# A chained attention and two expert layers on one core: the second weights' splits, the one-hots, the last tile and the last expert's gathers are moved

## The chip, the core and the metric

One Trainium2 chip, one of its cores, one launch. The metric is the device time of one execution in microseconds (us); lower is better. The profile below was taken by the hardware profiler in one execution of its own.

## What is computed

Three stages, each fed by the one before, all in float32 (inputs as numpy arrays):

```python
# 1. clustered attention: batch 2, 8 heads, 768 positions, 64 wide, 16 clusters a head
q_assign = argmax(q_n @ c_n.T); k_assign = argmax(k_n @ c_n.T)
scores = where(q_assign == k_assign, scale * q @ k.T, -1e9)
attn_out = softmax(scores) @ v
x = attn_out.transpose(0, 2, 1, 3).reshape(1536, 512)
# 2. experts, top 2 of 8, with noise on the gate
noisy = x @ w_gate + log1p(exp(x @ w_noise)) * noise
for each token, its two best experts e with softmax weight g:
    out += g * (relu(x @ w1[e]) @ w2[e])          # w1 512 x 1024, w2 1024 x 512
# 3. experts, top 1 of 8, at most 384 tokens an expert
probs = softmax(x @ w_gate2); e = argmax
out = probs[e] * (relu(x @ w1[e]) @ w2[e])        # tokens beyond the capacity stay 0
```

## The kernel before

**Arithmetic.** Float32 products are made of two rounded words: each operand is split into a high word (`hh`, `wh`, `xh`: a copy by ScalarE that rounds) and a low word (`hl`, `wl`, `xl`: VectorE subtracts the high one), and three matmuls (high x high, high x low, low x high) are added in one accumulator. So every weight that arrives (`raw`, 128 x 1024 at a time) is split by one ScalarE activation (L202) and one VectorE subtraction (L203). A "half" is one expert's w1 or w2; it has four such chunks. Half 0 is expert 0's w1, half 1 its w2, half 2 expert 1's w1, and so on. Four staging buffers hold raw chunks, three buffers of split words (`WB`) take the halves in turn.

**Attention.** 16 heads (2 batches of 8), each in six tiles of 128 queries, software-pipelined by a table of slots (`SLOTS`): scores, maximum, exponential, transposition, product with v into one accumulator `acc` in PSUM (half a head at a time, copied out to `oT` at L825), and `xback`, which turns the result back, scales it (`xp`) and adds the head's share of the gate logits to `LG`. In the last heads half 0 is split in pieces (`wneed0` at the steps listed in `WS`), the rows of the first job are gathered, and its first hidden chunk (`wide1` with f = 0) is made at a fixed step.

**Jobs.** Each expert is a job: gather the rows of its tokens by indirect DMA on GpSimd (`gathers`), turn and split them (`prep`), first matmul in eight hidden chunks of 128 (`wide1`, 12 matmuls each; ScalarE makes `hh`, VectorE `hl`), second matmul tile by tile of 128 rows (`second`, 24 matmuls of 512 columns over the eight hidden chunks), copy out (`y`), scatter by indirect DMA (`scatter`, L1195). Expert 0 is two jobs, `jobs[0]` with 256 rows of batch 0 and `jobs[1]` with 256 rows of batch 1; so is the last expert (jobs 8 and 9). Job 0 can run before batch 1 is routed.

**Routing of batch 1** (`route1(1)`) runs beside job 0 as a generator: job 0 calls `tick` after each group of matmuls, and a tick lets the generator emit so many steps (`us` times a pace; `PA` is the pace during job 0's first matmul, 3.0). It finds the two best experts of each token (A, L395), ranks the tokens by matmuls with triangular and all-one matrices (`ranks`, L298 to L303), turns ranks into slots, makes 12 pairs of one-hot matrices on VectorE (`ohp` 128 x 128, `ohv` 128 x 96, L321 and L323), multiplies them into a table on TensorE (L447) and finishes it (L449, then L329 to L337) to the token list `t1k`, which job 1's gathers (L1044) read. `K0` to `K3` space these steps.

Each engine takes its instructions in the order in which the program emits them. `wneed(n)` emits all splits that are left up to half n; `wneed0(n)` emits one. Until job 1's gathers are issued, no further weights are fetched (`rush`); the first fetch after that waits for the gathered rows. `early` issues the next job's gathers when its list is there; `fill` emits the next job's `prep`, once the planner's clock has passed the due time of its rows (`GT` after the gathers).

`first` fetches, for a last-expert job, the rows that its tokens got from their other expert (`y_dram`, L1214) and their gate weights (`g_dram`), which ScalarE multiplies (L1220). `combine` adds the two experts' rows of a token (L1652, L1653) and stores them (L1656) beside job 8. `every[-1]` is the last job of the third stage; its second and last tile stands in a branch on the count of its rows.

The lines of `work` that the change reorders:

```python
        early()
        if job.last:
            job.first()
...
                if job is jobs[0] and f % 2 == 0:
                    wneed0(1)
                tick(12 * job.n / 2400, PA if job is jobs[0] else 3.0)
...
        wneed(job.h + 1)
```

## Time and profile before

| | us |
|---|---|
| median of three runs | 857.37 (853.73 to 858.87) |
| the profiled execution | 849.86 |
| its span, first to last instruction | 848.1 |
| TensorE busy in it | 820.2 |
| VectorE, ScalarE, GpSimd busy | 540.1, 495.1, 287.9 |

Times in the views are counted from the span's start. PE is TensorE, DVE VectorE, ACT ScalarE, POOL GpSimd, SP SyncE; an engine's name with a q is its queue of instructions that only issue. A timeline row is start, duration, engine, source line, operation, output <- input, shape, count, and in brackets the engine's idle time just before it with what ended that. Matmuls overlap their neighbours, so the step from one start to the next is their cost, and a row's duration is longer than that.

### The profile page before, as it was taken

The numbers are of one execution on the slowest core, as the hardware profiler recorded it, in microseconds if no ns is written. First come the engines' busy times: TensorE is split into PE (matmuls) and PEld (weight loads), VectorE is DVE, ScalarE is ACT, GpSimd is POOL, SyncE is SP. The second block draws the span as 40 slices with busy tenths as digits, with TensorE's granted clock in tenths as the row PEclk, the third lists the DMA queues.
The fourth block names the chain that finished last, engine by engine and source line by source line (L and its number), as shares of the span: only waits on it lengthen the run. The fifth ranks groups of instructions, "written<-read, shape, count | busy, mean of one in ns | idle before, by whom it ended". The sixth has DMA issues, their size and how long they took to land. (4 is left out here: it accounts for less than half of the span.)

```text
span 848.1 us, 14830 instructions
## 1 busy us (share of the span) xinstructions
PE 820.2 (97%) x5350; PEld 733.6 (87%) x5350; DVE 540.1 (64%) x1104; ACT 495.1 (58%) x959; POOL 287.9 (34%) x488
## 2 busy tenths in 40 slices
PE   8999999999998989999999999999999999999997
PEld 6999999888987868989888897988997789888895
DVE  7998888889988666447444443536476548565370
ACT  7989889888888315435343343436254347555461
POOL 3565565667764031231302021124322122222210
PEclk9999999999999999999999999999999999999999
DMA  3125521411113034744644454438465529775250
GB/s 97 34 72 181 198 73 33 147 46 50 39 39 111 20 138 152 241 161 137 185 157 138 166 150 137 119 138 275 144 222 181 191 80 295 274 233 183 87 166 18
DMA packets 62181, 116.75 MB, mean 138 GB/s; under 512 B 13737, under 2 KB 25769, under 8 KB 62096
## 3 DMA queue, kind: packets, MB, share of 16 engines
q1 hardware_dynamic: 52832, 92.60, 34.4%
q0 software_dynamic: 9264, 23.06, 8.1%
q8 instruction: 47, 0.77, 0.4%
q14 instruction: 38, 0.31, 0.1%
HBM read 97.29 MB, written 23.74 MB: 143 GB/s over the span
## 5 line engine op out<-in xcount | busy, mean ns | idle before, releaser
L203 DVE TENSOR_TENSOR wl<-raw,wh 128x1024 fp32r<-128x1024 f32 x124 | 150.3, 1222 | 44.9 <-ACT wh L202 42.5
L1106 PE MATMUL l<-xh,wh 128*128 128x256 f32 (+1 forms) x508 | 156.0, 309 | 2.3 <-ACT xh L1087 0.9
L1106 PE MATMUL l<-xh,wl 128*128 128x256 f32 (+1 forms) x508 | 155.4, 308 | 0.2 <-DVE wl L203 0.2
L1106 PE MATMUL l<-xl,wh 128*128 128x256 f32 (+1 forms) x508 | 148.1, 307 | 0.0
L1151 PE MATMUL l<-wh,hh 128*128 128x512 f32 x328 | 134.9, 411 | 1.5 <-PEq L1343 0.5
L202 ACT ACTIVATE wh<-raw 128x1024 fp32r<-128x1024 f32 x124 | 129.0, 1054 | 7.9 <-DMA raw<-in_moe_w_dram 6.9
L1153 PE MATMUL l<-wh,hl 128*128 128x512 f32 x328 | 129.3, 394 | 0.0
L1152 PE MATMUL l<-wl,hh 128*128 128x512 f32 x328 | 129.0, 393 | 0.0
L1109 DVE SCALAR_TENSOR_TENSOR hl<-l,hh 128x256 fp32r<-128x256 f32 (+1 forms) x127 | 61.3, 484 | 98.6 <-ACT hh L1108 96.4
L1108 ACT ACTIVATE hh<-l 128x256 fp32r<-128x256 f32 (+1 forms) x127 | 55.0, 433 | 101.5 <-PE l L1106 99.6
L801 DVE TENSOR_TENSOR El<-et,Eh 128x384 fp32r<-128x384 f32 x192 | 99.7, 550 | 11.1 <-ACT Eh L800 8.1
L1106 PEld LDWEIGHTS l<-xh,wh 128*128 128x128 f32 x508 | 95.6, 188 | 5.8 <-issue 2.8
L1106 PEld LDWEIGHTS l<-xh,wl 128*128 128x128 f32 x508 | 95.4, 188 | 1.1 <-DVE wl L203 0.4
L769 DVE TENSOR_REDUCE nm<-st 128x1 f32<-128x768 f32 x96 | 91.3, 951 | 6.0 <-PE st L764 4.9
L1106 PEld LDWEIGHTS l<-xl,wh 128*128 128x128 f32 x508 | 93.7, 188 | 0.6
L800 ACT ACTIVATE Eh<-et 128x384 fp32r<-128x384 f32 x192 | 87.2, 493 | 10.5 <-PE et L795 10.2
L778 ACT ACTIVATE E<-st,nm 128x768 f32<-128x768 f32 x96 | 87.1, 907 | 7.6 <-DVE nm L769 7.6
L1195 POOL DMA_INDIRECT y_dram<-y,t1d x23 | 23.2, 1010 | 195.5 <-ACT y L1174 157.5
L1153 PEld LDWEIGHTS l<-wh,hl 128*128 128x128 f32 x328 | 61.6, 188 | 14.9 <-DVE hl L1123 0.3
L1151 PEld LDWEIGHTS l<-wh,hh 128*128 128x128 f32 x328 | 61.8, 188 | 14.6 <-issue 3.1
L795 PE MATMUL et<-identr,Er 128*128 128x128 f32 x576 | 70.9, 241 | 1.1 <-DVE El L801 1.0
L763 PE MATMUL st<-KB,QC 80*128 80x384 f32 x192 | 70.6, 367 | 1.2 <-ACT E L778 1.2
(331 smaller groups left out, 1527.5 us busy)
## 6 DMA issues: line engine op xcount, KB each, us to landing
raw<-in_moe_w_dram SPq DMA_DIRECT2D x128, 512.0 KB, 4.4
vraw<-in_v_dram SPq DMA_DIRECT2D x16, 192.0 KB, 2.5
x_dram<-xp SPq DMA_DIRECT2D x8, 384.0 KB, 3.2
out_dram<-xg SPq DMA_DIRECT2D x1, 3072.0 KB, 9.9
y_dram<-xg SPq DMA_DIRECT2D x1, 3072.0 KB, 9.9
part<-y_dram SPq DMA_DIRECT2D x12, 256.0 KB, 4.2
yt<-y_dram SPq DMA_DIRECT2D x12, 256.0 KB, 4.4
x_dram<-part POOLq DMA_DIRECT2D x12, 256.0 KB, 4.4
```

Source lines behind the costliest of these rows:

```text
L202: nc.scalar.activation(wh[:, cs], raw[0], AF.Copy)
L203: nc.vector.tensor_tensor(wl[:, cs], raw[0], wh[:, cs].bitcast(F32), op=OP.subtract)
L763: nc.tensor.matmul(ps, st["QC", i][:64 + C, js], st["KB", i][:64 + C, cs], start=True, stop=False)
L769: nc.vector.tensor_reduce(nm, ps, axis=AX.XY, op=OP.max, negate=True)
L778: made = nc.scalar.activation(E, st.pop(("S", i, j))[:, :, :HW], AF.Exp, bias=st.pop(("nm", i, j)), accum_out=st["Z", i][:, j:j + 1])
L795: ins = nc.tensor.transpose(ps[:, n * 128:(n + 1) * 128].bitcast(F32R), E[:, part, n * 128:(n + 1) * 128], identr)
L800: nc.scalar.activation(Eh[o], ps, AF.Copy)
L801: nc.vector.tensor_sub(El[o], ps, Eh[o].bitcast(F32))
L1106: nc.tensor.matmul(ps[:, :n], (w1l if k == 2 else w1h)[:, c, fs], (self.xl if k == 1 else self.xh)[:, c, :n], start=(m == 0), stop=(m == l ...
L1151: nc.tensor.matmul(ps[:rows], hh[:, f, cs], w2h[:, f, :], start=(f == 0), stop=False)
L1152: nc.tensor.matmul(ps[:rows], hh[:, f, cs], w2l[:, f, :], start=False, stop=False)
L1153: nc.tensor.matmul(ps[:rows], hl[:, f, cs], w2h[:, f, :], start=False, stop=(f == FC - 1))
```

## The change

1. Split weights are kept in tiles that hold half of the words of a half, high and low together (`wtile`, `Half`), and the tile for the first two chunks of half 1 is there from the start (`WB[1]`).
2. Job 0's first hidden chunk is emitted when the next to last half head of the attention is done, and the first two chunks of half 1 are split on either side of it; the third is split just ahead of the one-hots, the fourth just after the token table.
3. For batch 1 the ranks stand behind hidden chunk 5 (`FR`), the steps from the ranks to the one-hots are emitted in one go, and of the 12 pairs of one-hots six `ohv` are made on ScalarE, as relu(code - 2 code (lane - f)^2). The table matmuls stand behind the first four hidden chunks of both tiles in job 0's second matmul, which goes by parts of the hidden chunks (`second_turns`: four, two, two) and not tile by tile. The pace `PA` is 4.5.
4. For head 15 `xback` adds the gate logits first, on VectorE, and scales the rows after that.
5. The last tile of the last job is made in two column halves of 256; each is copied out by ScalarE and VectorE, 128 columns each, and scattered by itself.
6. In a last-expert job, `first` stands ahead of `early`.

The diff, cut to its core:

```diff
-    F0, FP, T0, PA = 1, (2, 4), 1.5, 3.0
-    K0, K1, K2, K3 = 10, 3, 1.5, 2
...
+    class Half:
+        def __init__(self, tiles, k, nch):
+            self.tiles, self.k, self.per = tiles, k, nch // 2
+        def __getitem__(self, key):
+            _, c, fs = key
+            w = self.tiles[c // self.per][:, self.k].rearrange("p (c f) -> p c f", c=self.per)
+            return w[:, c % self.per, fs]
+    def wtile(pool, p, n):
+        return pool.tile([128, 2, 2048], F32R, name=f"w{p}{n}")
+    WB = [[wtile(ring, p, 0) for p in "ab"], [wtile(ring, "a", 1)]]
...
             def op(cs=cs, raw=raw, g=g):
-                wh, wl = WB[buf]
-                W[n] = [w.rearrange("p (c f) -> p c f", c=nch) for w in (wh, wl)]
-                nc.scalar.activation(wh[:, cs], raw[0], AF.Copy)
-                nc.vector.tensor_tensor(wl[:, cs], raw[0], wh[:, cs].bitcast(F32), op=OP.subtract)
+                W[n] = [Half(WB[buf], p, nch) for p in range(2)]
+                wh, wl = [WB[buf][g // 2][:, p, cs] for p in range(2)]
+                nc.scalar.activation(wh, raw[0], AF.Copy)
+                nc.vector.tensor_tensor(wl, raw[0], wh.bitcast(F32), op=OP.subtract)
...
-    def one_hot(f, n, code, ncol):
-        oh = rt.tile([128, 128], F32R, name="ohp", bufs=4)
+    def one_hot(f, n, code, ncol, pool=None, minus=None):
+        pool, k = (pool, 2 * J) if pool else (my, 4)
+        oh = pool.tile([128, 128], F32R, name="ohp", bufs=k)
         nc.vector.tensor_scalar(oh, lane, f[:, 0, n:n + 1], None, op0=OP.is_equal)
-        val = rt.tile([128, ncol], F32R, name="ohv", bufs=4)
+        val = pool.tile([128, ncol], F32R, name="ohv", bufs=k)
+        if minus is not None:
+            far = pool.tile([128, ncol], F32, name="far", bufs=2)
+            nc.scalar.activation(far, lane[:, :ncol], AF.Square, scale=-1.0, bias=f[:, 1, n:n + 1])
+            nc.scalar.activation(val, far, AF.Relu, scale=minus, bias=code)
+            return oh, val
...
+        if b:
+            minus = hot.tile([128, J], F32, name="minus")
+            nc.gpsimd.tensor_scalar(minus, code1[:, b, :, 1], -2.0, None, op0=OP.mult)
...
-            yield K0
+        while b and st["f"] < FR:
+            yield
         ps = psum()
         ranks(ps, A, 0)
-        if b:
-            yield K1
         rs = rt.tile([128, J * E + E], F32, name="rs")
...
+        slots = split_slots(s2[:, 0:2].rearrange("p a j -> p (a j)"), 2 * J, "sf")
+        f = drain(slots) if b else (yield from slots)
...
-            for j in range(J + 1):
-                if j < J:
-                    hots += [one_hot(f, c * J + j, code1[:, b, j, c:c + 1], NC1) for c in range(2)]
-                    yield K2
-                for c in range(2 if j else 0):
-                    n = 2 * (j - 1) + c
-                    nc.tensor.matmul(ps2[:, :NC1], *hots[n], start=(n == 0), stop=(n == 2 * J - 1))
-            yield K3
+            wneed0(1)
+            for j in range(J):
+                hots += [one_hot(f, c * J + j, code1[:, b, j, c:c + 1], NC1, hot, minus[:, j:j + 1] if c else None) for c in range(2)]
+            for n in range(2 * J):
+                while st["pairs2"] < 1:
+                    yield
+                nc.tensor.matmul(ps2[:, :NC1], *hots[n], start=(n == 0), stop=(n == 2 * J - 1))
             nc.vector.tensor_add(st["tab0"], ps2[:, :NC1], st["tab0"])
-            yield
-            st["dst1"], st["tok1"] = yield from finish_table(st["tab0"], "t1", True)
+            st["dst1"], st["tok1"] = drain(finish_table(st["tab0"], "t1", True))
...
+            wneed0(1)
+            yield
...
+        def rows():
+            nc.vector.tensor_tensor(xp[:, :, h % 2, :], acc[:, :, 0:D], r.to_broadcast([128, J, D]), op=OP.mult)
+        def gates():
+            nc.vector.tensor_tensor(lt, acc[:, :, D:], r.to_broadcast([128, J, 16]), op=OP.mult)
+            if h:
+                (nc.vector if i == NBH - 1 else nc.gpsimd).tensor_tensor(LG, LG, lt, op=OP.add)
+        for part in (gates, rows) if i == NBH - 1 else (rows, gates):
+            part()
...
+            if self is every[-1] and t == len(self.main) - 1:
+                at = my.tile([128, 2], I32, name="halves")
+                c = self.col + t
+                nc.vector.tensor_scalar(at[:, 0:1], st[self.dst][:, c:c + 1], 1, None, op0=OP.logical_shift_left)
+                nc.vector.tensor_scalar(at[:, 1:2], at[:, 0:1], 1, None, op0=OP.bitwise_or)
+                for half in range(2):
+                    ds = slice(half * Dm // 2, (half + 1) * Dm // 2)
+                    ps = p2.tile([128, Dm], F32, name="l2")[:, ds]
+                    for f in range(FC):
+                        nc.tensor.matmul(ps[:rows], hh[:, f, cs], w2h[:, f, ds], start=(f == 0), stop=False)
+                        nc.tensor.matmul(ps[:rows], hh[:, f, cs], w2l[:, f, ds], start=False, stop=False)
+                        nc.tensor.matmul(ps[:rows], hl[:, f, cs], w2h[:, f, ds], start=False, stop=(f == FC - 1))
+                    y = my.tile([128, Dm], F32, name="y")[:, ds]
+                    g = self.gate[:rows, t:t + 1]
+                    q = Dm // 4
+                    nc.scalar.activation(y[:rows, :q], ps[:rows, :q], AF.Identity, scale=g)
+                    nc.vector.tensor_scalar(y[:rows, q:], ps[:rows, q:], g, None, op0=OP.mult)
+                    self.scatter(t, rows, y, at[:rows, half:half + 1])
+                return
...
+        def second_turns(self, hh, hl, pause, before):
+            ps = [p2.tile([128, Dm], F32, name="l2") for _ in self.main]
+            for part, fs in enumerate(((0, 1, 2, 3), (4, 5), (6, 7))):
+                while sum(n == self.h + 1 for n, _, _ in wops) > 2 - part:
+                    wstep()
+                w2h, w2l = W[self.h + 1]
+                for t, rows in self.main:
+                    cs = self.cols(t, rows)
+                    for f in fs:
+                        nc.tensor.matmul(ps[t], hh[:, f, cs], w2h[:, f, :], start=(f == 0), stop=False)
+                        nc.tensor.matmul(ps[t], hh[:, f, cs], w2l[:, f, :], start=False, stop=False)
+                        nc.tensor.matmul(ps[t], hl[:, f, cs], w2h[:, f, :], start=False, stop=(f == FC - 1))
+                        if f % 2 == 1 and f < FC - 1:
+                            if (part, t, f) == (0, 1, 3):
+                                st["pairs2"] = 1
+                            elif (part, t) == (1, 0):
+                                st["pairs2"] = 2
+                            pause()
+                    if part == 2:
+                        y = my.tile([128, Dm], F32, name="y")
+                        nc.scalar.activation(y, ps[t], AF.Copy)
+                        before()
+                        self.scatter(t, rows, y)
+                        pause()
...
+            to, at = self.out, st[self.dst][:rows, c:c + 1]
+            if half is not None:
+                to, at = to.rearrange("t (h d) -> (t h) d", h=2), half
...
-        early()
         if job.last:
             job.first()
+        early()
         for n in pre:
...
-                if job is jobs[0] and f % 2 == 0:
-                    wneed0(1)
+                if job is jobs[0]:
+                    st["f"] = f
                 tick(12 * job.n / 2400, PA if job is jobs[0] else 3.0)
         else:
             rest = job.tile1(0, hh, hl, tick, fill)
-        wneed(job.h + 1)
+        if job is not jobs[0]:
+            wneed(job.h + 1)
...
+        if job is jobs[0]:
+            job.second_turns(hh, hl, step, early)
+            early()
+            fill(False)
+            fill(False)
+        for t, rows in job.main if job is not jobs[0] else ():
...
-            if (i, t, s) == (NBH, 1, 3):
+            if done[0] == 2 * NBH - 1 and "begun" not in st:
+                st["begun"] = True
                 wneed(0)
+                wneed0(1)
...
                 for f in range(F0):
                     jobs[0].wide1(f, *st["first"])
+                wneed0(1)
...
-    for n in (1, 2):
-        WB.append([ring3.tile([128, 4096], F32R, name=f"w{p}{n}") for p in "hl"])
+    WB[1].append(wtile(ring3, "b", 1))
+    WB.append([wtile(ring3, p, 2) for p in "ab"])
+    hot = phase["first"].enter_context(tc.tile_pool(name="hot", bufs=1, side="right", reuse_waits="tile"))
```

## Rows read from the trace of the kernel before

**Rows 1.** The page's summary by engine: busy us, share of the span, instructions.

```profile
PE 820.2 (97%) x5350; PEld 733.6 (87%) x5350; DVE 540.1 (64%) x1104; ACT 495.1 (58%) x959; POOL 287.9 (34%) x488
```

**Rows 2.** Table of stretches: us, busy by engine, PEclk, DMA share, GB/s.

```profile
293.60:310.20 16.60, 14.57 (x75) 11.14 (x74) 13.95 (x68) 2.24 (x5) 3.07 (x3) 1.00 0.14 42
```

**Rows 3.** TensorE's timeline at the seam: start, us, line, count, [idle<-releaser].

```profile
278.73 0.44 PE L822 MATMUL acc<-Eh,vt 128*128 128x384 f32 x1 [0.68 <-ACT oT L825]
...
290.65 0.39 PE L1106 MATMUL l<-xh,wh 128*128 128x256 f32 x1 [0.59 <-DVE hl L1109]
...
293.57 0.20 PE L298 MATMUL rps<-A,below 128*128 128x48 bf16 x1
...
299.40 2.40 PE L447 MATMUL rps<-ohv,ohp 128*128 128x96 f32 x6 [1.07 <-DVE ohv L323]
...
304.51 0.46 PE L1151 MATMUL l<-wh,hh 128*128 128x512 f32 x1
...
310.18 1.34 PE L1085 MATMUL tp<-ident,xg 128*128 128x128 f32 x8
312.45 0.39 PE L1106 MATMUL l<-xh,wh 128*128 128x256 f32 x1 [0.92 <-ACT xh L1087]
```

**Rows 4.** VectorE's timeline at the seam.

```profile
282.64 0.56 DVE L842 TENSOR_TENSOR xp<-et,z 128x384 f32<-128x384 f32 x1 [3.59 <-PE et L836]
...
283.93 0.21 DVE L366 SCALAR_TENSOR_TENSOR ra<-LG 128x48 f32<-128x48 f32 x1 [0.56 <-POOL LG L846]
...
288.20 1.23 DVE L203 TENSOR_TENSOR wl<-raw,wh 128x1024 fp32r<-128x1024 f32 x1
...
296.68 0.21 DVE L404 COPY rs<-rps 128x56 f32<-128x56 f32 x1
...
298.73 0.29 DVE L321 TENSOR_SCALAR ohp<-lane,sf 128x128 fp32r<-128x128 bf16 x1
298.93 0.32 DVE L323 TENSOR_SCALAR ohv<-lane,sf,code 128x96 fp32r<-128x96 bf16 x1
...
304.72 0.26 DVE L449 TENSOR_TENSOR tab<-rps,tab 128x96 f32<-128x96 f32 x1 [0.41 <-PE rps L447]
...
305.57 0.21 DVE L337 TENSOR_SCALAR t1k<-t1d 128x96 int32<-128x96 int32 x1
```

**Rows 5.** GpSimd's timeline: the first gather of job 1's rows.

```profile
306.06 1.02 POOL L1044 DMA_INDIRECT xg<-x_dram,t1k  x1 [0.83 <-DVE t1k L337]
```

**Rows 6.** The view of tile xg, 300 to 330 us: time to landing.

```profile
DMA to landing us min/median/max: 3.2/3.9/6.0
```

**Rows 7.** ScalarE's timeline: the attention's last accumulator.

```profile
281.16 0.49 ACT L825 ACTIVATE oT<-acc 128x384 f32<-128x384 f32 x1 [2.49 <-PE acc L822]
```

**Rows 8.** ScalarE's groups by shape: busy us, mean ns, idle before.

```profile
L703 ACT ACTIVATE KB<-et 80x384 fp32r<-80x384 f32 x31 | 15.1, 486 | 4.6 <-PE et L694 4.5
...
L699 ACT ACTIVATE QC<-et,msc 80x384 fp32r<-80x384 f32 x16 | 9.3, 579 | 0.1
...
L1087 ACT ACTIVATE xh<-tp 128x128 fp32r<-128x128 f32 x6 | 1.7, 279 | 6.0 <-PE tp L1085 6.0
L919 ACT ACT_TABLE_LOAD x1 | 1.3, 1283 | 0.7 <-PEq L1759 0.7
```

**Rows 9.** SyncE's timeline in job 8: the first fetch of y_dram.

```profile
573.09 0.33 SPq L1638 DMA_DIRECT2D part<-y_dram  x1
```

**Rows 10.** GpSimd's timeline in job 8: job 9's first gather.

```profile
572.11 1.06 POOL L1044 DMA_INDIRECT xg<-x_dram,t1k  x1 [0.30 <-PE l L1106]
```

**Rows 11.** TensorE's timeline in job 8: job 9's first rows turned.

```profile
586.62 0.66 PE L1085 MATMUL tp<-ident,xg 128*128 128x128 f32 x4 [0.46 <-ACT x2T L1620]
```

**Rows 12.** Timeline of all engines at the last tile's end.

```profile
842.45 0.69 ACT L1172 ACTIVATE y<-l,xgate 128x512 f32<-128x512 f32 x1 [4.88 <-PE l L1153]
843.41 0.98 POOL L1195 DMA_INDIRECT out_dram<-y,u1d  x1 [4.56 <-ACT y L1172]
```

**Rows 13.** What the DMA queues moved, 835 to 848.1 in 40 slices.

```profile
GB/s 50 0 0 0 0 0 0 0 0 0 0 0 0 213 375 213 0 0 0 0 0 0 0 0 0 0 0 0 0 0 163 75 0 0 0 0 0 0 0 0
```

More of the change, by code (lines that the diff above doesn't have):

```diff
@@ L172 @@
     W = {}
-    WB = [[ring.tile([128, 4096], F32R, name=f"w{p}0") for p in "hl"]]
+    class Half:
[8 more added lines that the diff above has]
+    WB = [[wtile(ring, p, 0) for p in "ab"], [wtile(ring, "a", 1)]]
     wops = []
@@ L406, in route1 @@
         tot = rs[:, J * E:]
-        yield
+        if not b:
+            yield
         base = eoff1 if b == 0 else st["base"]
@@ L1191, in second_few, with scatter @@
             self.scatter(t, rows, y)
-        def scatter(self, t, rows, y):
+        def scatter(self, t, rows, y, half=None):
             c = self.col + t
+            to, at = self.out, st[self.dst][:rows, c:c + 1]
+            if half is not None:
+                to, at = to.rearrange("t (h d) -> (t h) d", h=2), half
             ins = nc.gpsimd.indirect_dma_start(
-                out=self.out, out_offset=bass.IndirectOffsetOnAxis(ap=st[self.dst][:rows, c:c + 1], axis=0),
-                in_=y[:rows], in_offset=None, bounds_check=self.out.shape[0] - 1, oob_is_err=False)
+                out=to, out_offset=bass.IndirectOffsetOnAxis(ap=at, axis=0),
+                in_=y[:rows], in_offset=None, bounds_check=to.shape[0] - 1, oob_is_err=False)
             for other in self.scats:
@@ L1324, in work @@
         wfill()
-        for t, rows in job.main:
+        if job is jobs[0]:
[4 more added lines that the diff above has]
+        for t, rows in job.main if job is not jobs[0] else ():
             if t and t == len(job.main) - 1 and job.tail:
@@ L1608 @@
     st["rush"] = True
+    st["f"] = st["pairs2"] = 0
     spawn(route1(1, mpsum))
@@ L1727, in after_last @@
         ring4 = pool("split", "ring4")
-        WB.append([ring4.tile([128, 4096], F32R, name=f"w{p}3") for p in "hl"])
+        WB.append([wtile(ring4, p, 3) for p in "ab"])
         P["split"] = (128, pool("split", "mxs"), pool("split", "mhs"))
```

29 lines of the change are left out of this document (14 added, 15 removed).

## The prediction

> **What bounds the kernel now.** I read the summary of busy time first [rows 1]: TensorE is busy 97% of the span, ScalarE, VectorE and GpSimd 58, 64 and 34%. So only places where TensorE stands still can give time back. The table of stretches, read next, puts the largest of them at the seam between the attention and the first expert layer: in the second matmuls of job 0, from 293.6 to 310.2 us, TensorE is busy 14.57 of 16.6 us, at a granted clock of 1.00 (2.4 GHz), gaps and all [rows 2].
>
> TensorE's timeline [rows 3] says what it waits for there. Ahead of the last half of the attention's value product it waits 0.68 us for ScalarE to empty the one accumulator. In job 0 it waits 0.59 us for a hidden chunk and 1.07 us for the first one-hot values; then six table matmuls take 2.4 us, at the pace of VectorE. Job 1's first matmul waits 0.92 us for its turned rows. VectorE's timeline [rows 4] shows why. The routing of batch 1 is one chain of small VectorE steps from 283.93 (L366) to 305.78 (end of the token table t1k), and the four splits of the second weights (L203, about 1.2 us each, the first at 288.20) are queued inside it. Job 1's rows are fetched the moment t1k is there [rows 5]. That chain and job 0's own matmuls end together (rows about 310 by their landing time [rows 6], TensorE free at 310.18), so both have to shrink.
>
> **The change, part by part.** Times are on the profile's axis.
>
> Tail of the attention. Job 0's first hidden chunk moves to just behind the matmul that fills the accumulator. TensorE then has 1.4 us of work while ScalarE empties it: -0.68. At head 15 the gate sums go first and their addition moves from GpSimd to VectorE. From the first of these steps at 282.64 to L366 took 1.29 us, 0.56 us of it idle for GpSimd [rows 4]; now it is two 96-wide steps (0.28 each, as L449 to the next) and the 384-wide one (0.48), 1.04: -0.25. The two splits that come here cost 2 x 1.06 us on ScalarE and 2 x 1.2 on VectorE. ScalarE has 2.49 us idle there [rows 7] and VectorE 3.59 [rows 4], against which I cost them at nothing; without that cover, up to 1 us. L366 starts at 283.0.
>
> Chain to the one-hots. Two L203, which pushed the chain back by 1.13 us each, are gone from before A (L395), and with the tick paced 4.5 in place of 3 one residual fewer (0.33) is queued in it. The ranks, which read A, began at 293.57; less 0.93, 2.27 and 0.33, A is there at 290.0. On TensorE chunks 1 to 5 run from 281.7 at 1.42 us each (chunks 6 and 7 took 2.92 up to 293.57 [rows 3]) to 288.8. The ranks now stand behind chunk 5, not chunk 7, so TensorE waits for A: 1.2 us, a new wait, with chunks 6 and 7 queued behind it. They end at 290.0 + 0.35 + 2.84 = 293.2. On VectorE two residuals follow A, then the steps from rs to the first one-hot, which took 298.73 - 296.68 = 2.05 us [rows 4]: 290.7 + 2.05 = 292.75. The third split (1.13) stands next: 293.9.
>
> One-hots. Before, 12 pairs of 0.44 us (ohp 0.20, ohv 0.24 to the next) were 5.3 us. Now VectorE keeps 12 ohp and 6 ohv: 3.84 us, done at 297.7. ScalarE makes six values by two activations each. No row shows Square. The nearest rows [rows 8]: a 128x128 activation is 0.28 us, and a per-partition operand adds 0.09 (L699 against L703). The Square is then 0.37, the Relu with two such operands 0.47, a pair 0.84 us at most, 0.56 at least if neighbours overlap. I take 0.83 because the second reads the first: 5.0 us, 292.75 + 5.0 = 297.75. Behind them on ScalarE stand hidden chunks 6 and 7, which only the last third of the second matmuls reads.
>
> Rows bear that split out: VectorE's ohv is 0.24 us where the pair on ScalarE is 0.83, yet both queues end together. The Trainium skill, "ScalarE: Activation LUTs", section Rules for kernel authors, speaks against it: for relu, mul and the like it says to use VectorE. By that rule the one-hots would end at 293.9 + 5.3 = 299.2, after TensorE gets there (298.8, next), and the gain would be 0.4 us less.
>
> Table and rows. The second matmuls now run both tiles by parts: four hidden chunks of each tile first, 24 matmuls at 0.2333 us (a tile's worth was 304.51 to 310.18 less a slower first one [rows 3]): 293.2 + 5.6 = 298.8. The 12 table matmuls then run unbroken, about 0.13 us each: 300.4. From there to the end of t1k took 305.78 - 304.72 = 1.06 us: 301.5, against 305.78. Rows are asked for 0.28 us later [rows 5] and land 3.2 to 3.9 us after that [rows 6]: 305.0 to 305.7. TensorE meanwhile does the middle part (2.8) and the first tile's last part (1.4): 304.6. The fourth split, queued behind t1k on VectorE, ends at 302.7, before 303.2 when it is read; if it were later, TensorE would wait for the difference. The planner puts the turning of the first rows here, so TensorE waits about 0.75 us (0.4 to 1.1), turns them (0.36), does the last 1.4 us, turns the second rows (0.4) and stands at 307.5. ScalarE copies y and the rows (0.6 each, the 0.69 of [rows 12] without its operand) before job 1 starts: 308.4, against 312.45. The seam gives **-4.0 us**. Its ends: -6.4 if the waits of 1.2, 0.75 and half of the last one don't come; -2.0 if the splits are not covered and the landing is a microsecond slower. The fetch of the next weights stands behind these rows as before and moves with them, so I see nothing later that gives this back.
>
> Last expert. The gathers of its first-layer rows now go ahead of those of job 9's rows in GpSimd's queue. They read y_dram, whose last scatter landed only at 573.05, where it freed a fetch on SyncE [rows 9]; before, gathers of x rows from 572.11 on covered that [rows 10]. So GpSimd waits about 1 us, and the stores of combined rows behind it, and the refills that wait on them, move back by that. Against it the gate rows come sooner to ScalarE, and perhaps the 0.46 us that TensorE waits behind ScalarE at 586.62 [rows 11] goes. Job 9's rows are asked for behind four more gathers of 1.3 us, by 579.9, and read at 586.6: covered even with 6.0 us, the longest landing of [rows 6]. Between -0.5 and +1.0; I take 0.
>
> End. The last tile's 24 matmuls of 512 columns (5.60 us) become 48 of 256 (0.118 each, as in the hidden chunks: 5.68): +0.1. The evacuation of 0.69 us [rows 12] becomes 128 columns on each of two engines, 0.28 + 0.09 = 0.37 [rows 8]: -0.32. GpSimd's 0.98 us [rows 12] stays (128 rows again). The last scatter's bytes took about two slices of 0.33 us [rows 13]; half of them, -0.3. The first half's scatter is issued some 2.5 us earlier and hides; the two index steps are done long before. Together **-0.5** (-0.8 to +0.3).
>
> Sum: -4.0 + 0 - 0.5 = -4.5 us. The profiled execution took 849.86 us (span 848.1), so 845.4 of its kind. The median of the three runs is 857.37, 7.5 above it, and the same difference gives **852.9**, 0.5% less. About 1% is what a measurement of this kernel can tell from no change.
>
> **Rivals.**
> Waits move. The ranks behind chunk 5 and the turning of rows inside the last part are both placed where TensorE gets there first. If A or the rows come a microsecond later than reckoned, each is paid one for one: -2, 855.4. For: both waits are already in my sum. Against: nothing else is queued on GpSimd or the DMA queues then.
>
> Slower: ScalarE changes its function tables. Place: between the Exp of L367, the Squares, the Relus and the Exp of L472. Price: 1.28 us each, the load in [rows 8]. Two loads hide while ScalarE waits for the slots, or cost up to 1.3. If every Square and every Relu brought one, 12 x 1.28 + 5.0 = 20.4 us from 292.75, so the last value would come at 313.1, where it came at 304.3: +8.8, less 0.5 at the end, 865.7. It decides from about 5 loads on (292.75 + 5.0 + 5 x 1.28 = 304.2). For it: no row shows Square. Against: this kernel mixes Exp, Copy, Relu and Identity over its whole span with few loads.
> The Trainium skill, "ScalarE: Activation LUTs", section Table sets: the hidden batching unit, names relu, copy, identity and abs among what every set holds, and not Square; it prices a switch at 2.66 us with its drain. No row here shows that drain; by it two switches would make 5.3 us, hidden in part.
>
> The end does nothing. If the last scatter's time is fixed and doesn't go by its bytes, and two evacuations cost two waits, the column halves are worth 0 to +0.3: 853.4 to 853.7.
>
> More. If neither new wait comes and the seam gives its full 6.4, with 0.5 at the end: 850.5.
>
> **How the numbers follow.** Forecast 0.60 (851 to 855), moved waits 0.20, the end alone failing 0.06, more 0.09, slower 0.05. The runs of before lie between 853.73 and 858.87, so a median can be off by some 2.5 us either way; with the bounds above the range is 848 to 857.5. Faster by over 1% (below 848.8) takes the larger gain and a low median: 0.11. Slower by over 1%: 0.04. Within: 0.85.
>
> **What would show it.** No L203 between L366 and A; TensorE waiting about 1 us ahead of L298; table matmuls no longer at 0.4 us each; t1k about 4 us earlier; job 1's first matmul at 308 to 309; no new table load; after 320 us every later row earlier by the same 4 us; two short evacuations at the end. I would be wrong if later stages gave the 4 us back, if the one-hots on ScalarE ended well after 298.8, or if the end were not shorter.

## The result and the profile after

The changed kernel takes **845.6 us** (median of 6 runs, 843.94 to 851.1) where the kernel before, timed beside it in 6 runs, takes 856.95: a ratio of 0.989, with an interval of 0.986 to 0.992. The prediction was 852.9, range 848.0 to 857.5; the gain is more than twice as large as forecast. The two profiled executions, on which the sum was made, differ by only 849.86 − 844.95 = 4.91 us, where the sum said 4.5. So the steps have to be read on the profile first, and then the gap between 4.9 and the medians explained. One run of the kernel before, at 986.47 us with a granted clock of 0.751, is left out of every figure below.

TensorE's timeline at the seam, after (start, us, engine, line, count, [idle before <- releaser]), answers to [rows 3]:

```profile
289.44 0.20 PE L313 MATMUL rps<-A,below 128*128 128x48 bf16 x1 [0.57 <-DVE A L419]
...
298.26 1.44 PE L475 MATMUL rps<-ohv,ohp 128*128 128x96 f32 x12
...
305.31 0.65 PE L1120 MATMUL tp<-ident,xg 128*128 128x128 f32 x4 [1.34 <-DMA xg<-x_dram,t1k]
...
308.53 0.74 PE L1141 MATMUL l<-xh,wa 128*128 128x256 f32 x4 [0.74 <-ACT xh L1122]
```

The ranks, at 293.57 before, start at 289.44, behind a short new wait for A. The table matmuls are one unbroken group of 1.44 us; the 1.07 us wait and the stutter behind it are gone. TensorE waits 1.34 us for rows, and job 1 starts at 308.53 where it started at 312.45: 3.92 us earlier. The rows come within the forecast (305.31, in 305.0 to 305.7); the wait is longer because TensorE stands ready at 303.97 and not at 304.6.

VectorE's and then ScalarE's timeline of the same stretch, after; they answer to [rows 4]:

```profile
282.50 0.20 DVE L390 SCALAR_TENSOR_TENSOR ra<-LG 128x48 f32<-128x48 f32 x1
...
289.18 0.21 DVE L419 TENSOR_TENSOR A<-oh 128x48 bf16<-128x48 f32 x1
...
291.98 1.23 DVE L218 TENSOR_TENSOR wb<-raw,wb 128x1024 fp32r<-128x1024 f32 x1
293.12 0.28 DVE L336 TENSOR_SCALAR ohp<-lane,sf 128x128 fp32r<-128x128 bf16 x1
...
296.71 0.28 DVE L336 TENSOR_SCALAR ohp<-lane,sf 128x128 fp32r<-128x128 bf16 x1
...
300.57 0.21 DVE L358 TENSOR_SCALAR t1k<-t1d 128x96 int32<-128x96 int32 x1
```

```profile
292.01 0.38 ACT L341 ACTIVATE far<-lane,sf 128x96 f32<-128x96 bf16 x1 [1.77 <-DVE sf L329]
292.48 0.47 ACT L342 ACTIVATE ohv<-far,code,minus 128x96 fp32r<-128x96 f32 x1
...
296.32 0.47 ACT L342 ACTIVATE ohv<-far,code,minus 128x96 fp32r<-128x96 f32 x1
```

No split (L218) stands between L390 and A. A value's two activations take 0.38 and 0.47 us, and six values take from 292.01 to 296.79, 0.80 us each; both queues are done near 297, before TensorE comes at 298.26. No table load stands among them; the kernel has two, as before, elsewhere.

The gather that follows t1k, after, answers to [rows 5]. It took 1.81 us, not 1.02, and so used up the 0.7 us by which t1k was there earlier than forecast (300.78 for 301.5):

```profile
301.05 1.81 POOL L1079 DMA_INDIRECT xg<-x_dram,t1k  x1 [20.35 <-DVE t1k L358]
```

The end, after, all engines, answers to [rows 12]:

```profile
837.32 0.28 PE L1195 MATMUL l<-wb,hl 128*128 128x256 f32 x1
837.69 0.37 ACT L1199 ACTIVATE y<-l,xgate 128x128 f32<-128x128 f32 x1 [2.35 <-PE l L1195]
838.09 0.35 DVE L1200 TENSOR_SCALAR y<-l,xgate 128x128 f32<-128x128 f32 x1 [2.37 <-ACT y L1199]
838.71 0.98 POOL L1278 DMA_INDIRECT out_dram<-y,halves  x1 [1.74 <-DVE y L1200]
```

VectorE starts its half when ScalarE's is over: the two short evacuations came one after the other, 0.75 us in all. One engine alone would have been quicker: between 0.37 us for 128 columns here and 0.69 for 512 in [rows 12], 256 columns come to about 0.48 (an estimate). From the start of the last matmul to the end of the span it is 843.2 − 837.32 = 5.88 us; before, 848.1 − 841.97 = 6.13.

### The profile page after: what moved, and what is told of

It is laid out like the page before. It is cut to its first block, busy times and chain, and to the rows that moved or that the text cites. A ratio compares the mean times of both kernels' runs of the same rounds, so it can differ in the third digit from the quotient of the medians.

```text
span 843.2 us, 14911 instructions
## 1 busy us (share of the span) xinstructions
PE 815.5 (97%) x5374; PEld 731.6 (87%) x5374; DVE 539.5 (64%) x1103; ACT 499.8 (59%) x972; POOL 292.6 (35%) x489
## 5 line engine op out<-in xcount | busy, mean ns | idle before, releaser
L1141 PE MATMUL l<-xh,wa 128*128 128x256 f32 (+1 forms) x508 | 125.3, 310 | 1.5 <-ACT xh L1122 0.7
L1141 PE MATMUL l<-xh,wb 128*128 128x256 f32 (+1 forms) x508 | 124.3, 307 | 0.3 <-DVE wb L218 0.3
L829 DVE TENSOR_TENSOR El<-et,Eh 128x384 fp32r<-128x384 f32 x192 | 99.8, 551 | 11.2 <-ACT Eh L828 8.1
L218 DVE TENSOR_TENSOR wa<-raw,wa 128x1024 fp32r<-128x1024 f32 x62 | 75.9, 1224 | 36.5 <-ACT wa L217 33.3
L1141 PEld LDWEIGHTS l<-xh,wa 128*128 128x128 f32 x508 | 88.9, 188 | 5.2 <-issue 2.8
L1141 PEld LDWEIGHTS l<-xh,wb 128*128 128x128 f32 x508 | 88.8, 189 | 0.8 <-DVE wb L218 0.5
L218 DVE TENSOR_TENSOR wb<-raw,wb 128x1024 fp32r<-128x1024 f32 x62 | 75.1, 1222 | 9.3 <-ACT wb L217 9.3
L1141 PE MATMUL l<-xl,wa 128*128 128x256 f32 (+1 forms) x254 | 75.5, 307 | 0.0
L1141 PE MATMUL l<-xl,wb 128*128 128x256 f32 (+1 forms) x254 | 75.4, 307 | 0.0
L217 ACT ACTIVATE wa<-raw 128x1024 fp32r<-128x1024 f32 x62 | 65.3, 1054 | 4.1 <-DMA raw<-in_moe_w_dram 3.3
L848 PE MATMUL acc<-El,vt 128*64 128x384 f32 x192 | 66.8, 350 | 0.0
```

Source lines behind the costliest of these rows:

```text
L217: nc.scalar.activation(wh, raw[0], AF.Copy)
L218: nc.vector.tensor_tensor(wl, raw[0], wh.bitcast(F32), op=OP.subtract)
L829: nc.vector.tensor_sub(El[o], ps, Eh[o].bitcast(F32))
L848: nc.tensor.matmul(acc[:64, :HW], vt[:, 0], El[:, t], start=False, stop=(t == J - 1), skip_group_check=True)
L1141: nc.tensor.matmul(ps[:, :n], (w1l if k == 2 else w1h)[:, c, fs], (self.xl if k == 1 else self.xh)[:, c, :n], start=(m == 0), stop=(m == l ...
```

## The experiments

Ratios are to the kernel before on the same chip, with their intervals. The chips differ more than the kernels do: the kernel before has medians near 855 us on three of them and near 864.7 on two. "Mean clock" is the granted clock of a run, averaged over the runs of a kernel. "Old seam" and "changed seam" say which order of the work between the attention and job 1 a kernel has; a "fall" is a stretch at a granted clock of 0.50 (1.2 GHz) in place of 1.00 (2.4 GHz). The chip of the first comparison is not on record; by its times it is taken to be of the 855 kind.

| kernel | chip kind | median us | ratio | mean clock |
|---|---|---|---|---|
| a0_before, before again | 855 | 855.65 | 1.000 [0.998, 1.002] | 0.9892 |
| a1_seam, only the seam | 855 | 846.52 | 0.990 [0.987, 0.993] | 0.9967 |
| a2_halves, only the column halves | 855 | 855.11 | 1.000 [0.998, 1.002] | 0.9873 |
| a3_first, only the gather order | 855 | 855.24 | 0.999 [0.997, 1.002] | 0.9896 |
| c0_before | 855 | 855.05 | 1.001 [0.999, 1.003] | 0.9898 |
| c1_after, the changed kernel | 855 | 848.1 | 0.992 [0.989, 0.995] | 0.9928 |
| c2_fill, before with the gap filled | 855 | 853.45 | 0.997 [0.995, 0.999] | 0.9952 |
| c3_fill2, after with the second routing filled | 855 | 846.22 | 0.990 [0.987, 0.993] | 0.9960 |
| e1_first, as a3_first | 855 | 855.35 | 0.999 [0.997, 1.002] | 0.9895 |
| e2_noswap, after with the old gather order | 855 | 848.44 | 0.991 [0.988, 0.994] | 0.9930 |
| b1_fill, as c2_fill | 865 | 864.01 | 0.999 [0.997, 1.002] | 0.9904 |
| b2_gap, after with a wait added | 865 | 856.35 | 0.991 [0.987, 0.994] | 0.9872 |
| b3_dve, after, all one-hots on VectorE | 865 | 852.52 | 0.984 [0.981, 0.987] | 0.9918 |
| b4_order, after, two orders moved | 865 | 852.55 | 0.985 [0.981, 0.989] | 0.9910 |
| d0_before | 865 | 863.81 | 1.000 [0.997, 1.003] | 0.9873 |
| d1_after, the changed kernel | 865 | 853.35 | 0.987 [0.982, 0.991] | 0.9915 |
| d2_dve, as b3_dve | 865 | 854.56 | 0.988 [0.984, 0.992] | 0.9888 |
| d3_fill2, as c3_fill2 | 865 | 851.26 | 0.984 [0.980, 0.989] | 0.9932 |

**Which part gives the gain.** First the kernel before unchanged, so that its runs and profile stand beside the others.

> The kernel before, unchanged, against itself. The change measured -11 us by medians (856.95 to 845.6), but only -4.9 between the two profiled executions (849.86 to 844.95). Theory A (clock): executions of the kernel before differ by a stretch at a lower granted clock, so runs of it spread over some 850 to 859 us, the longer ones with a mean clock lower by about 0.007 (0.007 x 850 = 6 us), and a profile of a long one shows where. Theory B (the profiled execution was a lucky one by something else): the same spread with the clock the same in all. Theory C (sessions): within one session the spread is under 2 us and the ratio to itself is 1.000.

Then the changed kernel without the column halves and with the old order of the gathers:

```
-            if self is every[-1] and t == len(self.main) - 1:
+            if False and self is every[-1] and t == len(self.main) - 1:
...
+        early()
         if job.last:
             job.first()
-        early()
```

> The change without the column halves of the last tile and without the new order of the last expert's gathers. Between profiles I reckon -4.0 (seam) against before. Theory A with the lost clock at the seam: -8 to -11 by medians. Theory A with the lost clock elsewhere, or C: -4 by medians.

And each of those two parts alone put into the kernel before: the branch of `second` that computes the last tile by halves, with its `scatter`; and

```
-        early()
         if job.last:
             job.first()
+        early()
```

> The kernel before with the column halves of the last tile alone. By my sum -0.5 (ratio 0.9994; -0.8 to +0.3). If the missing 6 us hung on this part: -6.

> The kernel before with the last expert's gathers ahead of the next job's alone. By my sum 0 (-0.5 to +1.0). If the missing 6 us hung on this part: -6.

The seam alone gives 0.990, 8.6 us by the medians, as theory A forecast for lost clock at the seam; the halves and the order alone give nothing that can be measured. That the gain is no more than a lucky timing is ruled out too: before against itself is 1.000. Its twelve runs bear theory A out: 853.94 to 858.98 us, with the clock between 0.983 and 0.994 and lower in the long ones. But the profile of before taken here is not the one that the prediction was made from. The table of stretches of a0_before (from:to, us, TensorE busy (count), granted clock, DMA share, GB/s), and TensorE's timeline in it:

```profile
290.00:300.00 10.00, 8.31 (x60) 1.00 0.00 0
300.00:302.00 2.00, 1.70 (x6) 0.69 0.00 0
302.00:310.00 8.00, 8.00 (x22) 0.50 0.15 42
310.00:312.00 2.00, 2.00 (x8) 0.75 0.53 178
312.00:320.00 8.00, 6.77 (x49) 1.00 0.75 279
```

```profile
298.36 0.40 PE L1153 MATMUL l<-wh,hl 128*128 128x512 f32 x1
299.83 2.53 PE L447 MATMUL rps<-ohv,ohp 128*128 128x96 f32 x6 [1.07 <-DVE ohv L323]
...
303.15 0.63 PE L1153 MATMUL l<-wh,hl 128*128 128x512 f32 x1
303.58 0.63 PE L1151 MATMUL l<-wh,hh 128*128 128x512 f32 x1
304.00 0.63 PE L1152 MATMUL l<-wl,hh 128*128 128x512 f32 x1
...
311.39 0.40 PE L1151 MATMUL l<-wh,hh 128*128 128x512 f32 x1
311.62 0.40 PE L1152 MATMUL l<-wl,hh 128*128 128x512 f32 x1
```

About 1 us after the end of the 1.07 us wait, while six table matmuls take 2.53 us, the granted clock goes from 1.00 to 0.50, by these slices from about 300.8 to 311.0. The second matmuls then start 0.43 us apart, not 0.233. The same stretch in the execution that the prediction used, with the same wait:

```profile
300.00:302.00 2.00, 1.51 (x7) 1.00 0.00 0
302.00:310.00 8.00, 7.59 (x36) 1.00 0.28 82
310.00:312.00 2.00, 1.44 (x10) 1.00 0.17 36
```

That gives the theory that the rest of the study tests: the change takes away not only idle time, but in some executions the fall of the clock behind it. The rival: the schedule alone.

**Fill the gap, or add one.** In the kernel before, throw-away matmuls keep TensorE at work until the one-hots come; nothing else moves:

```
+                    if n == 0:
+                        idle1 = pt.tile([128, DC, 128], F32, name="tp")
+                    for _ in range(9 if n == 0 else 2 if n < 6 or n > 9 else 0):
+                        nc.tensor.matmul(idle1[:, 0:2, :], onesb, onesb[:, None, :].to_broadcast([128, 2, 128]), start=True, stop=True)
                     nc.tensor.matmul(ps2[:, :NC1], *hots[n], start=(n == 0), stop=(n == 2 * J - 1))
```

> The kernel before with idle TensorE time filled: 9 matmuls of 256 columns on constants ahead of the first table matmul, 2 ahead of eight of the others, into an accumulator that nobody reads. The routing chain and everything else stay. In the unchanged kernel's new profile TensorE waits 1.07 us there, then goes at the pace of the one-hots, and from about 301.4 to 310.8 us the granted clock is 0.50. Theory A (that pause brings the clock down, and the change gains some 4 us by not having it): no stretch at 0.50 there, -3 to -4.5 us by medians (ratio 0.995 to 0.9965), most at 850 to 852. Rival (the clock falls there for another reason, or the gain is the schedule's): 0 to +1.

The opposite: the changed kernel with its one-hots held back by eight additions on VectorE.

```
+            for _ in range(8):
+                nc.vector.tensor_tensor(xgs[2], xgs[2], xgs[2], op=OP.add)
             for j in range(J):
                 hots += [one_hot(f, c * J + j, ...) for c in range(2)]
```

> The changed kernel with eight VectorE additions of 528 columns (about 0.6 us each, of zeros) ahead of the one-hots, so that the one-hots end some 4.8 us later and TensorE waits for them as before. From VectorE 296.9 + 4.8 = 301.7 against 298.3 where TensorE gets there: +2 to +3.5 us of waiting. Theory A: the clock falls after it, +4 more, so +6 to +8 over the changed kernel (852 to 853). Rival: +2 to +3.5 alone (848 to 849).

On that chip the fill gave 0.1% and not the 0.35 to 0.5% expected of it. The added wait did bring the fall; TensorE's timeline of b2_gap:

```profile
304.30 3.72 PE L477 MATMUL rps<-ohv,ohp 128*128 128x96 f32 x12 [1.19 <-DVE ohv L344]
307.82 0.76 PE L1245 MATMUL l<-wb,hh 128*128 128x512 f32 x1
308.38 0.63 PE L1246 MATMUL l<-wb,hh 128*128 128x512 f32 x1
...
311.95 0.40 PE L1247 MATMUL l<-wb,hl 128*128 128x512 f32 x1
...
313.69 0.66 PE L1122 MATMUL tp<-ident,xg 128*128 128x128 f32 x4
...
316.91 0.74 PE L1143 MATMUL l<-xh,wa 128*128 128x256 f32 x4 [0.74 <-ACT xh L1124]
```

From the ranks (294.13) to job 1 (316.91) it takes 22.78 us, where nine profiles with the changed seam take 18.97 to 19.14. But this is not the price of the fall. The table starts 10.17 us after the ranks, in the profile after 8.82, and takes 3.72 us in place of 1.44: 3.63 us more by the wait and the pace of the one-hots. From the table's end to job 1 it is 8.89 us with the fall and 8.83 without, because the fall (some 3 us) stands where TensorE would else have waited 1.34 us for the rows; that wait is gone. The median is 3.8 us above that of b3_dve beside it (the changed kernel itself was not run on that chip): nearer the rival's 2 to 3.5 than theory A's 6 to 8. The run shows that a fall can follow such a wait, not what a fall costs.

The fill was run again beside the changed kernel:

> The kernel before, unchanged, against itself: ratio 1.000 within 0.3%. Clock theory: its profile shows the granted clock near 0.5 for about 9 us from some 2 us behind the start of the table matmuls, and there the matmuls of the second layer step at 0.43 us in place of 0.233. Schedule theory: the granted clock at that place is 1.00, as in the execution that the prediction was made from.

> The changed kernel, unchanged, beside the other three. Both theories: 0.987 to 0.991 of the kernel before. Clock theory: the mean granted clock of its runs is some 0.004 above that of the kernel before, and at equal clock the two differ by 4 to 5 us. Schedule theory: equal clocks, and 8 to 10 us between the two at equal clock.

> The kernel before with TensorE kept at work on throw-away matmuls while it waits for the one-hots; they leave the order and the length of everything else as it was. Once more, with the changed kernel beside it. Clock theory: the clock is 1.00 through the seam in its profile; 2 to 4 us less than the kernel before by the medians, its mean granted clock 0.003 to 0.005 higher. Schedule theory: nothing gained, 0 to 1 us more.

The changed kernel is at 0.992, just outside the 0.987 to 0.991 that both theories gave it. Its clock is 0.0030 higher, and at equal clock it stands 4.4 to 5.3 us lower, as by the clock theory (0.0030 taken as 2.6 us, 0.0030 × 855, or as 1.6, by how the times of the runs go with their clock; both ways are told in the next section).

The fill gives 0.28%, 0.07 to 0.49, at a mean clock 0.0054 higher; by the medians it is 1.4 us, by the means 1.6 ± 0.7 (on the chip of b1_fill 1.1 ± 1.0). That is the sign of the clock theory and less than its 2 to 4 us. The profiles suggest why: c0_before has the wait of 1.07 us and no fall of the clock (1.00 from 300 to 312). Of seven profiles with the old seam and no fill, three have it (a0_before, a2_halves, a3_first) and four do not (the one of the prediction, c0_before, d0_before, e1_first). From the ranks to job 1 the four take 18.83 to 18.88 us, the three 22.45, 22.55 and 21.40; the two with the fill 18.83 and 18.85. So a fall there costs 2.6 to 3.7 us, 3.28 in the mean, and neither profile with the fill has one, at no cost of its own. With three falls in seven that is 3.28 × 3/7 = 1.4 us on the average. My 2 to 4.5 had put it in most executions.

How often the fall comes is not settled. All three profiles that have it were taken on one chip, and the four without it on others (that of the prediction's is not on record), though the kernel before has a mean clock of 0.989 to 0.990 on each chip of the 855 kind. And the 0.0054 by which the fill raises the mean clock is 0.0054 × 855 = 4.6 us of full-speed time, as much as one fall of 9 us at half the clock loses: that would be a fall in nearly every execution, where the profiles have three in seven. Its gain in time agrees with the profiles.

The Trainium skill, "TensorE: Matmul & The Clock Gate", section What's actually happening, says that the window of activity by which this clock is set runs freely and does not start anew with the kernel. The seven profiles fit that, and do not show it, as the chip differs too: the same wait of 1.04 to 1.07 us meets a fall in three and none in four.

**One-hots on ScalarE.** The changed kernel with all of them on VectorE, first alone and then beside the changed kernel:

```
-                hots += [one_hot(f, ..., NC1, hot, minus[:, j:j + 1] if c else None) for c in range(2)]
+                hots += [one_hot(f, ..., NC1, hot, None) for c in range(2)]
```

> The changed kernel with all 24 one-hots on VectorE. They start at 293.1 and would end at 293.1 + 12 x 0.44 = 298.4, where TensorE gets to the table at 298.26: +0.1 to +0.4 us, and a clock that may fall if the wait is long enough. If ScalarE's help is worth what it takes off VectorE: +1.4.

> The changed kernel once more, beside the next two on one chip. Ratio 0.988 to 0.993 to the kernel before by both theories. Clock theory: no fall of the clock between 290 and 312 us in its profile. At equal mean clock it stands 4.5 us below the kernel before if the terms of the prediction are all, 6 if the excess of 1 us seen on two chips is real.

> The changed kernel with all one-hots on VectorE, now beside the changed kernel. The prediction's step: 12 pairs of 0.44 us end about 0.4 us after TensorE gets there, so 0.4 us more than the changed kernel, 0 to 0.9. Rival: in the profile after, the ScalarE values end at 296.8 and TensorE comes at 298.3, so a VectorE end at 299 adds up to 0.8 us of wait, and if the clock falls behind that wait 1 to 4 us more by the median.

TensorE's timeline of d2_dve:

```profile
297.67 0.20 PE L313 MATMUL rps<-A,below 128*128 128x48 bf16 x1 [0.57 <-DVE A L419]
306.49 1.44 PE L475 MATMUL rps<-ohv,ohp 128*128 128x96 f32 x12
313.53 0.66 PE L1120 MATMUL tp<-ident,xg 128*128 128x128 f32 x4 [1.34 <-DMA xg<-x_dram,t1k]
```

From the ranks to the table it is 8.82 us, in d1_after 302.38 − 293.56 = 8.82 as well. The last pair leaves VectorE at 306.7, while the twelve table matmuls, begun at 306.49, are on their way: it comes just in time. This split of the one-hots is worth nothing here; 854.56 against 853.35 is within what six runs tell. The rule of the Trainium skill that the prediction weighed ("ScalarE: Activation LUTs", Rules for kernel authors: VectorE for relu and mul) would have lost nothing.

**The remaining waits of the seam.** The ranks behind chunk 6, and job 1's rows turned 2 us later in the planner's time:

```
-    F0, FP, T0, PA, FR = 1, (2, 4), 1.5, 4.5, 5
+    F0, FP, T0, PA, FR = 1, (2, 4), 1.5, 4.5, 6
...
-                self.at = clock["now"] + GT
+                self.at = clock["now"] + GT + (2 if self is jobs[1] else 0)
```

> The changed kernel with the ranks behind hidden chunk 6 in place of 5 (TensorE waited 0.57 us for A) and the turning of job 1's first rows behind the last part of the second tile (it waited 1.34 us for them). A is there at 289.4 and chunk 6 ends at 290.1, so no wait; the one-hots end 0.65 us later, at 297.6, and TensorE gets there at 297.7. Job 1 at 307 in place of 308.5: -1.0 to -1.6 us. If the waits only move on to the one-hots: 0.

The waits for A and for the first rows are gone, but they moved on, to the second rows (0.55 us) and to job 1:

```profile
316.97 1.10 PE L1141 MATMUL l<-xh,wa 128*128 128x256 f32 x4 [1.80 <-issue]
```

From the routing's first VectorE step (L390, at 291.03) to job 1 it takes 25.94 us, in b3_dve 25.91 and in the profile after 26.03. So the rival held, 0 in place of −1.0 to −1.6, and 852.55 is the time of b3_dve, and of the changed kernel on the other chip of that kind. Its profile has a fall of the clock at 225 to 235 us, in the attention, and one of some 3 us at job 1's start, behind the wait of 1.80 us. That fall begins only at job 1, so the gain was lost before it.

**The same pattern further on.** In the second routing TensorE waits in the same way, 0.85 us for the input of its ranks and 1.26 us for a one-hot. The changed kernel with throw-away matmuls there (six ahead of the ranks, and ahead of the later one-hots):

```
+        if b:
+            idle2 = pt.tile([128, DC, 128], F32, name="tp")
+            for _ in range(6):
+                nc.tensor.matmul(idle2[:, 0:2, :], onesb, onesb[:, None, :].to_broadcast([128, 2, 128]), start=True, stop=True)
...
+            if b and t == 4:
+                idle3 = pt.tile([128, DC, 128], F32, name="tp")
+            for _ in range({4: 9, 5: 3, 6: 2, 7: 2}.get(t, 0) if b else 0):
+                nc.tensor.matmul(idle3[:, 0:2, :], onesb, onesb[:, None, :].to_broadcast([128, 2, 128]), start=True, stop=True)
```

> The changed kernel with throw-away matmuls in the waits of the second routing (0.85 us ahead of the ranks, 1.26 us ahead of its second one-hot), where TensorE is idle in the same way. If drops of the clock behind that stall cost the changed kernel time in some of its executions, its median falls by 0.5 to 2 us against the changed kernel and its mean granted clock is higher; if not, it is the same within 0.3%, or up to 0.5 us longer.

> The kernel before once more, for one more profile of it: the clock falls at the table matmuls of the seam in three of the five profiles of it and of its variants that change nothing there. Clock theory: ratio 1.000 within 0.3%; if its profile has the fall, the span is 3 to 5 us above one without any fall of the clock. Schedule theory: no tie between the fall and the span.

> The changed kernel with throw-away matmuls in the waits of the second routing, once more. On the chip before it stood 1.4 us (means) below the changed kernel with an uncertainty of about 0.9. Clock theory: again 0.5 to 2 us below, mean granted clock 0.001 to 0.004 higher. Schedule theory: the same within 0.2%.

Beside the changed kernel it is 1.9 and 2.1 us less by the medians on two chips, with a mean clock higher by 0.0032 and 0.0017. The means differ by 1.35 ± 0.95 and 2.4 ± 1.2 us, together 1.8 ± 0.75: likely, and not certain. In d1_after the clock falls there (0.83 in 660 to 680 us); in d3_fill2 and c3_fill2 it does not, and in c1_after it did not either. Of the eight profiles of changed kernels without this fill and without an added wait, four have a fall between 650 and 680 us (b3_dve, b4_order, d1_after, e2_noswap). On each of its two chips this is the fastest of the versions run. The prediction on d0_before, a longer span with the fall, was not put to the test, as its profile has none at the seam.

**The two chips where the change gives more.** There the ratio is 0.987, just outside the 0.988 to 0.993 expected of d1_after; on the others it is 0.989 to 0.992. The profiles of before have TensorE busy only 15.8 of 20 us from 580 to 600 (d0_before 15.85, b1_fill 15.77, both with a mean clock of 0.91 there), those of the changed seam 17.95 to 19.24; on the other chips the old seam has 18.2 to 19.4, but 17.21 in a2_halves, again with 0.91. The last two runs were to tell whether the order of the gathers does that:

> The kernel before with only the order of the last expert's gathers changed, once more, for the chips where the kernel before takes 864 to 865 us: there its profiles show TensorE waiting about 4 us between 585 and 594 us, 2.3 of them for combined rows, where the profiles on the chips of 855 us show 1 us. If the new order removes that wait: 1.5 to 3 us less than the kernel before on such a chip, and 0 within 1.5 on a chip of 855 us, as before. If the wait has another cause: no difference on either.

> The changed kernel with the gathers of the last expert's first rows put back behind those of job 9. On a chip of 864 us: if the swap is worth 2 to 3 us there, the ratio to the kernel before is 0.989 to 0.991 in place of 0.987; on a chip of 855 us it is 0.989 to 0.992, as of the changed kernel. If the swap does nothing, the ratio is that of the changed kernel on either.

(e2_noswap puts `early()` back ahead of `job.first()`.) They fell on a chip of 855 us, where the order again is worth nothing that the times show (0.999 alone; 0.991 without it). The profiles there speak against the order rather than for it: with the changed seam TensorE is busy 19.74 of these 20 us in the old order (a1_seam; e2_noswap too, at a clock of 0.89) and 18.18 to 18.45 in the new one (the profile after, c1_after, c3_fill2). For the other kind this stays open.

## Why the prediction was wrong, by its own steps

**Most terms held.** The tail: chunk 0 covers the 0.68 us wait, and L390 starts at 282.50 (283.0 forecast). A: the ranks go at 289.44 behind a 0.57 us wait (290.0, 1.2). One-hots: ScalarE 0.80 us a value for the 0.83 taken, done at 296.8 (297.75). Table: 298.26 (298.8), unbroken. Rows: a wait of 1.34 where I took 0.75 with 1.1 as the upper end; the gather of 1.81 us was not in the sum, but t1k came 0.7 us early, so the rows were in time and TensorE was ready sooner than reckoned. Job 1: 308.53 (308.4), so the seam gave 3.92 where the sum had 4.0, by errors of half a microsecond that cancel. Last expert: from the last scatter into y_dram (566.38, 4.54 us earlier than in the profile before) to the first of the third stage (653.00, 3.55) the lead falls by 1.0, the upper end of −0.5 to +1.0, where I took 0. End: 0.25 in place of 0.5, since the halves' evacuations run in sequence (0.37 + 0.35, where I took 0.37). Table loads, the slow rival, did not come.

That the sum is 4.91 against 4.5 is in part luck. The lead did not stay at 4: it grew by 0.6 between job 1 and 566 us, fell by 1.0 in the last expert, and grew again by 0.8 up to the scatter at 788.79 and by 0.5 from there on. Of these only the last expert (at 0) and the end's part were in the sum. Most of the 0.8 belongs to the column halves: between the scatters at 760.88 and 788.79 it is 27.9 us in all eleven profiles with them, a2_halves among them, and 28.5 to 28.7 in all nine without. TensorE waits as long in both, but its 256-column matmuls there stand 0.114 us apart in the profile after and 0.119 in a1_seam; why is open. The medians do not resolve it (a2_halves: 1.000, 0.998 to 1.002).

**The step that failed** is the last: "The median of the three runs is 857.37, 7.5 above it, and the same difference gives **852.9**". It took the one profiled execution as a sample of the others shifted by a constant. That execution had a granted clock of 0.997 and 1.00 across the whole seam, while the runs of before, 94 of them on the 855 us chips, have a mean clock of 0.9896 and a median of 855.25. Of the 7.5 us, 2.1 were the draw of three runs (857.37 for 855.25). The other 5.4 went with a clock lower by 0.0074, which is 4.0 to 6.3 us by the two ways of the next paragraph: largely lost clock, and part of it lost behind the very wait that the change removes, so it did not carry over. No rival said so, although the gap was in the table of times.

**What stands in its place.** On the 855 us chips the changed kernel has a median of 846.99 (14 runs) and a mean clock of 0.9934: 8.3 us less than before. The difference in clock of 0.0038 is 0.0038 × 855 = 3.2 us of TensorE time; by how the time of the runs of one kernel on one chip goes with their clock (some 5.3 us for 0.01, a line through all runs about their own means) it is 2.0. With the 4.9 of the schedule that is 6.9 to 8.1 of 8.3. The 4.9 is the difference of two single executions; a second pair with equal falls, e1_first and c1_after (each one at 20 us and no other before the end), differs by 5.6. Of the clock's part, some 1.1 to 1.6 us sit at the seam by the two fills, with an uncertainty of 0.7 to 1.0, and 1.4 by the count of falls; that the rest comes from falls elsewhere is only argued. Outside the seam the stretches at 0.50 add up to 8.8 us an execution in the seven profiles with the old seam and 6.8 in the nine with the changed one, too few to tell apart. The 11.35 us of the first comparison are these 8.3 and a draw of six runs each on the fortunate side: 856.95 for 855.25, 845.6 for 846.99. On the 864 us chips 864.6 − 853.35 = 11.2 us were gained at a clock difference of 0.0046, worth 2.5 to 4.0 by the same two ways: 2.3 to 3.8 us more than schedule and clock account for. The waits at 580 to 600 us fit that in size; why they come there stays open.

## What to carry to other kernels

Before a sum is moved from a profiled execution to the median of runs, look at what separates the two: here the granted clock of each run did, and the gap of 7.5 us was a cost that the change itself acts on. An idle microsecond of TensorE, with short matmuls at another engine's pace behind it, can cost several more in the executions where the clock falls (2.6 to 3.7 here), unless a later wait takes the loss up, as in b2_gap; price it over several profiles of the same kernel, not one. Where such a wait cannot be removed, throw-away matmuls in it are a cheap try.

## What the runs showed of the hardware

- The granted clock fell to 0.50 for some 10, 10 and 7 us (a0_before, a2_halves, a3_first) beginning 1 to 3.5 us after the end of a wait of 1.04 to 1.07 us, while or just after six short matmuls went at VectorE's pace. It did so in three of seven executions with the same schedule there, all three on one chip, and at that place in none of nine without the wait.
- ScalarE and VectorE emptied their columns of one accumulator in sequence: VectorE, idle for 2.37 us, began at ScalarE's end. The Trainium skill, "PSUM — Partial Sum Buffer", section PSUM bank collisions raise a hardware error, says that the compiler's scheduler makes two engines that touch the same bank and partitions wait for each other, reads included; the trace agrees (838.09 behind 837.69 + 0.37).
- The same kernel has medians of 855 and of 864.7 us on different chips, far beyond the spread of one chip's medians. In all eight profiles of the slower kind TensorE waits more for ScalarE in the attention, ahead of the matmuls of `xback` (1.4 to 3.5 us, 3.5 of it at L836 in d0_before; 0.4 in the profile of the prediction and in all of the other kind). In d0_before ScalarE also stands still for 3.6 us at 588 us for a releaser that the trace calls remote.
